# Decode attention over a 4096-token window with a gated mixer: the order of the work behind the last unit's scores

## The chip, the cores and the metric

The kernel runs on one core of one Trainium2 chip. The metric is the device time of one execution in microseconds (us). The kernel before takes 219.3 us, the median of three runs (219.18 to 219.53). A change under about 0.2% (0.44 us) can't be told from none in a measurement of this kernel.

## The reference, cut to what matters

Two batches, one new token each (B = 2, D = 512), 32 query heads on 8 key/value heads of 128 dimensions, float32 throughout. Only the last W = 4096 keys and values of each cache are read.

```python
xn = layernorm(x)
q = (xn @ wq) per head
scores = q . k[last 4096] * 128**-0.5
p = softmax(scores)
o = p @ v[last 4096]
s = o (all heads side by side, 4096) @ wo          # 4096 x 512
z = gelu(xn @ w_in); z1, z2 = halves; z2 = layernorm(z2)
g = silu((z1 * (w_sp * z2 + b_sp)) @ w_out)
out = x + s * g
```

What has to be read is some 89 MB: wq 8 MB, w_in 3.5 MB, w_out 1.8 MB, the windows of keys and of values 32 MB each, and wo 8 MB.

## The kernel before, in words

**Units.** The attention is cut into eight units: batch b (0 or 1) times four pairs of key/value heads. A unit reads 4 MB of keys and 4 MB of values, 128 partitions by 8192 numbers. The last unit (n = 7) is called `last`, and the one before it is `prev` at the end (n = 6).

**Transfers.** All large loads go through one ring of four 4-MB slots in SBUF, and all are issued by SP, in the order of a list: wq, w_in, w_out, then keys of unit n and values of unit n-1 by turns, the values of unit 7, and then wo in pieces of 16, 8, 4, 1, 1, 1 and 1 blocks (a block is 512 numbers on each partition, 256 KB). `advance(slot)` (lines 93 to 100) marks a slot free in the program and issues what now fits; the issue waits on the chip for the last reader of the place that it overwrites. The 16 blocks go to the slot of unit 5's values, the 8 to that of unit 7's keys, and the 4 and the four single ones to that of unit 6's values.

**One unit** (loop of lines 499 to 526). VectorE (DVE) turns the keys in four transposes (`turn`, tiles `kt`). `scores` makes 16 matmuls on TensorE (PE) into the PSUM bank `sh`, ScalarE (ACT) copies it to `shs`, and `by_group_of_keys` regroups it with one matmul to the bank `s`. `share_max` takes a maximum per partition on DVE (`m`, `mg`), and one small matmul spreads it over the partitions that share a head (bank `mo`); `shift` makes the negative maximum `nb` of it (`mx`, `nb`); `probs` is the exponential on ACT (`p`, with its sums); `probs_t` transposes `p` to `pT` on DVE. `weigh`, in the last unit of a batch only, makes the reciprocal sums (`ls`, `lr`, a one-column matmul into `mo`, `wd`). `values` makes 16 matmuls of `pT` with the values, four at a time in the four column groups of the array, into the bank `acc`; `scale_out` multiplies four quarters of `acc` by a mask (tile `o`, one buffer; four ACT instructions, or two on ACT and two on DVE for `last`), and `collect` adds `o` with one matmul into the bank `col` of all units.

**The program's order is each engine's order.** The wrapper `InOrder` (lines 27 to 39) keeps every engine's instructions as written, so all of them have line 37 in the profile, and tiles tell them apart. Waits between engines are put in by the framework. One float32 matmul of the program is two MATMUL rows of the trace.

**The loop is one unit behind itself**: while the keys of unit u are turned, unit u-1 goes through maximum, exponential and transpose, and its values follow the scores of u.

**The end.** After the loop, `last` goes alone through `share_max` to `weigh`. Then come the first eight of its values, `gather` (DVE sums `col` over its four column blocks to `hq`, one matmul to the bank `oT`), the other eight values, `scale_out`, `divide` (by the sums, into the tile `oT`) and `collect_last` (bank `ol`, a reduction and a division). Then the projection with wo (lines 541 to 558): 28 blocks into the bank `part`, copied by ACT to `parts`, blocks 28 and 29 into the bank `so`, `parts` spread into `so`, blocks 30 and 31 into `so`. Each piece of wo is waited for before its first block. DVE forms `res` in two steps, and SP stores it.

Of the kernel before, what the change touches and what calls it, by code (L numbers as in the profile page):

```python
# [16 lines left out]
G = 4  # L17
# [4 lines left out]
def ap(t, offset, dims):  # L22

    return bass.AP(tensor=t.tensor, offset=t.offset + offset, ap=[list(t.ap[0])] + [list(d) for d in dims])
# [18 lines left out]
def kernel(  # L43
# [15 lines left out]
    B, _, D = x.shape  # L59
# [9 lines left out]
    NU = B * HKV // 2  # L69
    J = 2 * W // P  # L70
    JC = 512 // 32
# [21 lines left out]
    def advance(*slots):  # L93
        for n in slots:
            free[n] = True
        while queue and all(free[n] for n in queue[0][1]):
            load, at = queue.pop(0)
            for n in at:
                free[n] = False
            load(ring[:, at[0] * SLOT : (at[-1] + 1) * SLOT], at[0])  # L100
# [4 lines left out]
    def bank(name, tag):  # L105
        return ps.tile([P, 512], F32, tag=tag, name=name, bufs=BANKS[tag])
# [35 lines left out]
    for n in range(NU):  # L142
        u = Unit()
# [223 lines left out]
    def form_gate():  # L367
        dve.tensor_scalar(gate, y, -1.0, 80.0, op0=ALU.mult, op1=ALU.min)
        act.activation(gate, gate, AF.Exp)
        dve.tensor_scalar_add(gate, gate, 1.0)  # L370
        dve.reciprocal(gate, gate)
        dve.tensor_mul(gate, gate, y)


    def turn(u, m):

        u.kt[m] = sb.tile([P, JC, DH], F32, tag="kt", name=f"kt{u.n}_{m}", bufs=KTB)
        dve.transpose(
            u.kt[m].rearrange("p j d -> p (j d)"), u.k[:, JC * m : JC * m + JC, :].rearrange("p j d -> p (j d)")
        )  # L380

    def scores(u):

        u.sh = bank(f"sh{u.n}", "sh")
        for dq in range(4):
            for m in range(NCH):
                pe.matmul(
                    u.sh[32 * m : 32 * m + 32, :], q_of(u, dq), u.kt[m][:, :, 32 * dq : 32 * dq + 32],
                    start=(dq == 0), stop=(dq == 3),
                )  # L390
        u.shs = sb.tile([P, 512], F32, tag="shs", name=f"shs{u.n}", bufs=1)
        act.activation(u.shs, u.sh, AF.Copy)

    def by_group_of_keys(u):

        u.s = bank(f"s{u.n}", "s")
        pe.matmul(u.s, regroup, u.shs, start=True, stop=True)

    def share_max(u):
        m2 = sb.tile([P, 2], F32, tag="m2", name=f"m2_{u.n}")  # L400
        dve.tensor_reduce(m2, ap(u.s, 0, [[1, 2], [2, 256]]), axis=AX.X, op=ALU.max)
        mg = sb.tile([P, 2, G * NCH], F32, tag="mg", name=f"mg{u.n}")
        dve.tensor_mul(mg, ap(m2, 0, [[1, 2], [0, G * NCH]]), spot.rearrange("p a g m -> p a (g m)"))
        u.mo = bank(f"mo{u.n}", "mo")
        dve.tensor_add(mg[:, 0], mg[:, 0], mg[:, 1])
        pe.matmul(u.mo[:, : G * NCH], same_r, mg[:, 0], start=True, stop=True)

    def shift(u):

        mx = sb.tile([P, 1], F32, tag="mx", name=f"mx{u.n}")  # L410
        dve.reduce_max(mx, u.mo[:, : G * NCH], axis=AX.X)
        u.nb = sb.tile([P, 2], F32, tag="nb", name=f"nb{u.n}")
        dve.scalar_tensor_tensor(u.nb, ap(mx, 0, [[0, 2]]), -SCALE, negm, op0=ALU.mult, op1=ALU.add)
# [3 lines left out]
    def probs(u):  # L417

        u.p = sb.tile([P, 512], F32, tag="p", name=f"p{u.n}")
        if u.w == 0:  # L420
            sums[u.b] = sb.tile([P, NU // B, 2], F32, tag="l", name=f"l{u.b}")
        for a in range(2):
            act.activation(
                ap(u.p, a, [[2, 256]]), ap(u.s, a, [[2, 256]]), AF.Exp,
                bias=u.nb[:, a : a + 1], scale=SCALE, accum_out=sums[u.b][:, u.w, a : a + 1],
            )

    def probs_t(u):
        u.pT = sb.tile([P, JC, 32], F32, tag="pT", name=f"pT{u.n}")
        dve.transpose(u.pT.rearrange("p j r -> p (j r)"), u.p)  # L430

    def weigh(u):

        if u.w < NU // B - 1:
            return
        ls = sb.tile([P, NU // B], F32, tag="ls", name=f"ls{u.b}")
        dve.tensor_reduce(ls, sums[u.b], axis=AX.X, op=ALU.add)
        lr = sb.tile([P, NU // B, 8, 4], F32, tag="lr", name=f"lr{u.b}")
        dve.tensor_mul(lr, ap(ls, 0, [[1, NU // B], [0, 8], [0, 4]]), ap(rowr, 0, [[0, NU // B], [1, 8], [0, 4]]))
        pe.matmul(u.mo[:, 32:33], lr.rearrange("p w r e -> p (w r e)"), ones[:, 0:1], start=True, stop=True)  # L440
        dve.reciprocal(wd[:, u.b : u.b + 1], u.mo[:, 32:33])

    def values(u, js=range(JC)):
        if js[0] == 0:
            u.acc = bank(f"acc{u.n}", "acc")
        for j in js:
            c = j % G
            pe.matmul(
                u.acc[32 * c : 32 * c + 32, :], u.pT[:, j, :], u.v[:, j : J : JC, :],
                start=(j < G), stop=(j >= JC - G),  # L450
            )

    def scale_out(u):
        u.o = sb.tile([P, 4, DH], F32, tag="o", name=f"o{u.n}", bufs=1)
        for jj in range(4):
            o, acc, m = u.o[:, jj, :], u.acc[:, jj * DH : (jj + 1) * DH], diag[:, jj : jj + 1]
            if u is units[-1] and jj >= 2:
                dve.tensor_scalar_mul(o, acc, m)
            else:
                act.activation(o, acc, AF.Copy, scale=m)  # L460
# [3 lines left out]
    def collect(u, end=NU // B - 1):  # L464

        if u.n == 0:
            col[0] = bank("col", "col")
        r = slice(32 * u.b, 32 * u.b + 32)
        pe.matmul(
            col[0][r, :], sel[:, 24 - 8 * u.w : 56 - 8 * u.w], u.o.rearrange("p j d -> p (j d)"),  # L470
            start=(u.w == 0), stop=(u.w == end),
        )

    def gather(b):

        hq = sb.tile([P, 32], F32, tag="hq", name=f"hq{b}")
        by_d = col[0][32 * b : 32 * b + 32, :].rearrange("p (j d) -> p d j", j=NCH)
        for e in range(4):
            dve.reduce_sum(hq[32 * e : 32 * e + 32, :], by_d[:, 32 * e : 32 * e + 32, :], axis=AX.X)
        t = bank(f"oT{b}", "acc")[:, :32]  # L480
        pe.matmul(t, perm, hq, start=True, stop=True)
        return t

    def divide(b, t, r=slice(0, P)):
        dve.tensor_scalar_mul(oT[r, :, 16 * b], t, wd[r, b : b + 1])
# [11 lines left out]
    last = units[-1]  # L497
    prev = None
    for u in units:
        turn(u, 0)  # L500
        if u.n == NU // B + 1:
            divide(0, gather(0))
        turn(u, 1)
        if prev is not None:
            share_max(prev)
        else:
            form_gate()
        turn(u, 2)
        if prev is not None:
            shift(prev)  # L510
            probs(prev)
        turn(u, 3)
        advance(u.slot["k"])
        if prev is not None:
            probs_t(prev)
            weigh(prev)
        scores(u)
        if prev is not None:
            values(prev, range(G))
        by_group_of_keys(u)  # L520
        if prev is not None:
            values(prev, range(G, JC))
            scale_out(prev)
            advance(prev.slot["v"])
            collect(prev, prev.w if u is last else NU // B - 1)
        prev = u
    share_max(last)
    shift(last)
    probs(last)
    probs_t(last)  # L530
    weigh(last)
    early = slice(0, 32 * last.w)
    values(last, range(8))
    t = gather(last.b)
    values(last, range(8, JC))
    scale_out(last)
    divide(last.b, t[early, :], early)
    collect_last(last)
# [52 lines left out]
```

## Time and profile before

| what | value |
|---|---|
| time, median of three runs | 219.3 us (219.18 to 219.53) |
| time of the profiled execution | 219.93 us |
| span in it, first to last instruction | 218.1 us |
| mean granted TensorE clock | 0.863 of full speed |
| PE / DVE / ACT busy | 62% / 49% / 14% of the span |
| DMA queue of SP | 95.8% of 16 engines' span, 410 GB/s over the span |

The profile shows one execution, in us from the span's start. "Idle before" is the time that an engine stood still ahead of an instruction, with what ended it. The chain of waits goes back from the last instruction to what released each step. The granted clock is the share of full speed that TensorE had; in this trace it is either 1.00 or 0.50 at any moment.

### The profile page before, as it was taken

The numbers are of one execution on the slowest core, as the hardware profiler recorded it, in microseconds if no ns is written. First come the engines' busy times: TensorE is split into PE (matmuls) and PEld (weight loads), VectorE is DVE, ScalarE is ACT, GpSimd is POOL, SyncE is SP. The second block draws the span as 40 slices with busy tenths as digits, with TensorE's granted clock in tenths as the row PEclk, the third lists the DMA queues.
The fourth block names the chain that finished last, engine by engine and source line by source line (L and its number), as shares of the span: only waits on it lengthen the run. The fifth ranks groups of instructions, "written<-read, shape, count | busy, mean of one in ns | idle before, by whom it ended". The sixth has DMA issues, their size and how long they took to land.

```text
span 218.1 us, 2001 instructions
## 1 busy us (share of the span) xinstructions
PE 134.6 (62%) x794; PEld 36.2 (17%) x794; DVE 106.8 (49%) x161; ACT 31.1 (14%) x88; POOL 4.2 (2%) x21
## 2 busy tenths in 40 slices
PE   0010895417286698697782099358869638929593
PEld 0010221111011121121210032012112111203221
DVE  1040016348685968569309904394990396122201
ACT  2030000151201102213020101201221201130101
POOL 6010000000000000000000000000000000000000
PEclk9999997966959769999997559959999957995998
DMA  9889999999999999999999998999999999999950
GB/s 385 385 385 411 442 407 453 448 409 458 409 451 415 451 415 448 409 457 403 463 400 463 403 463 385 476 391 475 388 463 403 463 403 457 406 457 394 407 224 1
DMA packets 3788, 89.52 MB, mean 410 GB/s; under 512 B 434, under 2 KB 450, under 8 KB 964
## 3 DMA queue, kind: packets, MB, share of 16 engines
q1 hardware_dynamic: 3772, 89.40, 95.8%
q8 instruction: 6, 0.10, 0.2%
q14 instruction: 2, 0.02, 0.0%
q10 hardware_dynamic: 8, 0.00, 0.0%
HBM read 89.40 MB, written 0.00 MB: 410 GB/s over the span
## 4 chain that ended last, share of the span: by engine, by line
PE 35%; DMA 31%; DVE 25%; ACT 5%; issue 2%; ACTq 0%; DVEq 0%
DMA ring<-in_A_k_cache_dram 21%; DVE kt L37 16%; DMA ring<-in_A_wq_dram 10%; PE sh L37 9%; PE acc L37 8%; PE q_ps L37 5%; PE part L37 3%; PE z L37 2%; PE s L37 2%; ACT o L37 2%; PE y L37 2%; PE col L37 1%; DVE m L37 1%; PE mo L37 1%; DVE gate L37 1%
## 5 line engine op out<-in xcount | busy, mean ns | idle before, releaser
L37 DVE STREAM_TRANSPOSE kt<-ring 128x2048 f32<-128x2048 f32 x32 | 73.0, 2297 | 35.1 <-DMA ring<-in_A_k_cache_dram 30.6
L37 PE MATMUL sh<-kt,qbd 128*32 128x512 f32 x256 | 52.3, 733 | 12.3 <-DVE kt L37 11.5
L37 PE MATMUL acc<-ring,pT 128*32 128x512 f32 x256 | 38.1, 638 | 0.0
L37 PEld LDWEIGHTS sh<-kt,qbd 128*32 128x32 f32 x256 | 10.3, 128 | 47.9 <-DVE kt L37 22.7
L37 PE MATMUL q_ps<-ring,xnT 128*32 128x512 f32 x64 | 10.0, 795 | 7.4 <-DMA ring<-in_A_wq_dram 7.4
L37 ACT ACTIVATE o<-acc,diag 128x128 f32<-128x128 f32 x30 | 8.6, 368 | 37.0 <-PE acc L37 37.0
L37 PE MATMUL col<-o,sel 128*32 128x512 f32 x14 | 7.3, 602 | 9.3 <-ACT o L37 9.3
L37 ACT ACTIVATE p<-s,nb 128x256 f32<-128x256 f32 x16 | 7.6, 488 | 37.3 <-DVE nb L37 37.3
L37 PEld LDWEIGHTS acc<-ring,pT 128*32 128x32 f32 x256 | 8.9, 114 | 20.7 <-issue 20.6
L37 ACT ACTIVATE shs<-sh 128x512 f32<-128x512 f32 x8 | 4.8, 597 | 52.0 <-PE sh L37 52.0
L37 PE MATMUL mo<-mg,same_r 128*128 128x16 f32 x16 | 3.8, 313 | 13.1 <-DVE mg L37 13.1
L37 PE MATMUL xnT_ps<-ident,xn 2*128 2x2 f32 x4 | 0.6, 252 | 14.7 <-DVE xn L37 14.7
L37 PE MATMUL s<-shs,regroup 128*128 128x512 f32 x16 | 9.0, 643 | 0.8 <-ACT shs L37 0.8
L37 DVE STREAM_TRANSPOSE qT<-q_ps 128x512 f32<-128x512 f32 x2 | 1.4, 718 | 15.5 <-PE q_ps L37 15.3
L37 DVE TENSOR_REDUCE m<-s 128x2 f32<-128x512 f32 x8 | 5.3, 666 | 6.0 <-PE s L37 6.0
L37 PE MATMUL part<-ring,oT 128*32 128x512 f32 x56 | 6.2, 594 | 0.7 <-DVE oT L37 0.7
L37 PEld LDWEIGHTS mo<-mg,same_r 128*128 128x128 f32 x16 | 3.0, 234 | 19.2 <-DVE mg L37 13.7
L37 DVE STREAM_TRANSPOSE pT<-p 128x512 f32<-128x512 f32 x8 | 5.4, 674 | 1.1 <-ACT p L37 1.1
L37 PE MATMUL mo<-ones,lr 128*128 128x1 f32 x4 | 1.2, 363 | 7.7 <-DVE lr L37 7.7
L37 PE MATMUL y<-ring,hT 128*32 128x512 f32 x14 | 3.3, 993 | 3.8 <-DVE hT L37 3.8
L37 ACT ACT_TABLE_LOAD x4 | 5.1, 1283 | 0.8 <-PEq L577 0.7
L37 PEld LDWEIGHTS q_ps<-ring,xnT 128*32 128x32 f32 x64 | 2.7, 139 | 13.9 <-issue 13.9
(114 smaller groups left out, 61.8 us busy)
## 6 DMA issues: line engine op xcount, KB each, us to landing
ring<-in_A_k_cache_dram SPq DMA_DIRECT2D x8, 4096.0 KB, 19.7
ring<-in_A_v_cache_dram SPq DMA_DIRECT2D x8, 4096.0 KB, 24.4
ring<-in_A_wo_dram SPq DMA_DIRECT2D x1, 4096.0 KB, 30.5
ring<-in_B_w_in_dram SPq DMA_DIRECT2D x1, 3584.0 KB, 16.9
ring<-in_A_wo_dram SPq DMA_DIRECT2D x1, 2048.0 KB
ring<-in_B_w_out_dram SPq DMA_DIRECT2D x1, 1792.0 KB, 20.8
ring<-in_A_wo_dram SPq DMA_DIRECT2D x1, 1024.0 KB
ring<-in_A_wo_dram SPq DMA_DIRECT2D x4, 256.0 KB, 18.8
```

Source lines behind the costliest of these rows:

```text
L37: return self.tc.keep_in_program_order(call(*args, **kwargs))
```

## The change

In the last pass of the loop, `prev`'s remaining twelve values, its scaling and its collection no longer stand inside the loop. Behind the regrouping of the last unit's scores four of these values are left, then comes `share_max(last)` to `probs(last)`, then `prev`'s last eight values and the release of its slot, then the transpose and the sums of `last`. `prev`'s `scale_out` stands behind these, and its `collect` between the first and the second eight values of `last`. `gather` moves behind the second eight.

```diff
         if prev is not None:
             values(prev, range(G))
         by_group_of_keys(u)
+        if u is last:
+            break
         if prev is not None:
             values(prev, range(G, JC))
             scale_out(prev)
             advance(prev.slot["v"])
-            collect(prev, prev.w if u is last else NU // B - 1)
+            collect(prev)
         prev = u
+    values(prev, range(G, 8))
     share_max(last)
     shift(last)
     probs(last)
+    values(prev, range(8, JC))
+    advance(prev.slot["v"])
     probs_t(last)
     weigh(last)
+    scale_out(prev)
+    values(last, range(8))
+    collect(prev, prev.w)
     early = slice(0, 32 * last.w)
-    values(last, range(8))
+    values(last, range(8, JC))
     t = gather(last.b)
-    values(last, range(8, JC))
     scale_out(last)
     divide(last.b, t[early, :], early)
     collect_last(last)
```

On PE, from the regrouping of the last unit's scores (`s_800`) to the last unit's output (`ol`), before (`acc_795` is the bank of `prev`, `acc_847` that of `last`, `mo_829` with 16 columns the maximum, with one column the sums):

```order
L37 MATMUL s_800<-shs_793,regroup 128x512
L37 MATMUL acc_795<-ring,pT_774 32x512 x12
L37 MATMUL col<-o_814,sel 32x512
L37 MATMUL mo_829<-mg_827,same_r 128x16
L37 MATMUL mo_829<-ones,lr_843 128x1
L37 MATMUL acc_847<-ring,pT_839 32x512 x8
L37 MATMUL oT_861<-hq_856,perm 128x32
L37 MATMUL acc_847<-ring,pT_839 32x512 x8
```

The same place in the changed kernel (`acc_795` is still `prev`, `acc_846` is `last`):

```order
L37 MATMUL s_800<-shs_793,regroup 128x512
L37 MATMUL acc_795<-ring,pT_774 32x512 x4
L37 MATMUL mo_810<-mg_808,same_r 128x16
L37 MATMUL acc_795<-ring,pT_774 32x512 x8
L37 MATMUL mo_810<-ones,lr_837 128x1
L37 MATMUL acc_846<-ring,pT_833 32x512 x8
L37 MATMUL col<-o_841,sel 32x512
L37 MATMUL acc_846<-ring,pT_833 32x512 x8
L37 MATMUL oT_869<-hq_864,perm 128x32
```

The matmul of the maximum now stands behind four of `prev`'s values where it stood behind twelve and the collection; the collection stands between the two halves of `last`'s values, and the matmul of `gather` behind both.

On ACT, from the copy of the last unit's scores on (`p` is the exponential of `last`, `o` from `acc_795` the scaling of `prev`):

```order
 L37 ACTIVATE shs_793<-sh_776 128x512
-L37 ACTIVATE o_814<-acc_795,diag 128x128 x4
-L37 ACTIVATE p_836,l_626<-s_800,nb_834 128x256 x2
-L37 ACTIVATE o_871<-acc_847,diag 128x128 x2
+L37 ACTIVATE p_817,l_626<-s_800,nb_815 128x256 x2
+L37 ACTIVATE o_841<-acc_795,diag 128x128 x4
+L37 ACTIVATE o_871<-acc_846,diag 128x128 x2
```

The exponential of `last` now stands ahead of `prev`'s scaling. The order on DVE, POOL and SP stays as it was.

## The prediction

> **What bounds the kernel now.** I read the page's slices first, then the transfers at the end, then the chain of waits backwards from the store, then the granted clock by windows. DMA's row of the page:
>
> ```profile
> DMA  9889999999999999999999998999999999999950
> ```
>
> The DMA engines are busy in 38 of 40 slices, so the transfers set when everything arrives. The question is how much work is left behind the last of them. First a window at the end (columns: stretch, its us, busy us of PE, PEld, DVE, ACT, POOL, clock, DMA share, GB/s), then SP's issues with their times, each followed by the row of the transfers that gives its us from issue to landing (the values of unit 7, and four loads of wo):
>
> ```profile
> 212.00:213.00 1.00, 1.00 (x16) 0.26 (x8) 0.00 (x0) 0.00 (x0) 0.00 (x0) 1.00 0.00 0
> ```
>
> ```profile
> L37 SPq DMA_DIRECT2D ring<-in_A_v_cache_dram x1: 535/535/535, 163.3 to 163.3; - x1
> ring<-in_A_v_cache_dram SPq DMA_DIRECT2D x1, 4096.0 KB, 29.1
> 171.60 0.33 SPq L37 DMA_DIRECT2D ring<-in_A_wo_dram  x1
> ring<-in_A_wo_dram SPq DMA_DIRECT2D x1, 4096.0 KB, 30.5
> 191.19 11.21 SPq L37 DMA_DIRECT2D ring<-in_A_wo_dram  x5
> L37 SPq DMA_DIRECT2D ring<-in_A_wo_dram x2: 424/428/432, 192.0 to 192.5; - x2
> ring<-in_A_wo_dram SPq DMA_DIRECT2D x2, 256.0 KB, 18.8
> L37 SPq DMA_DIRECT2D ring<-in_A_wo_dram x1: 328/328/328, 202.1 to 202.1; - x1
> ring<-in_A_wo_dram SPq DMA_DIRECT2D x1, 256.0 KB, 10.0
> ```
>
> So unit 7's values are there at 163.3 + 29.1 = 192.4, the first 16 blocks of wo at 171.6 + 30.5 = 202.1, and the last block at 202.1 + 10.0 = 212.1. The two single blocks before it land 18.8 behind 192.0 and 192.5, at 210.8 and 211.3. The row of five at 191.19 begins with the pieces of 4 and 1 and ends with the issue at 202.1. Between 202.1 and 210.8 the engines carry 8 + 4 + 2 blocks, 3.7 MB, at a nearly even rate; my estimate by bytes is 207.0 for the piece of 8 and 209.5 for the piece of 4. Now the longest steps of the chain of waits from 188 on (start, us, what):
>
> ```profile
> 188.41 2.76 PE acc L37 x24
> 191.25 1.15 ACT o L37 x4
> 192.45 1.04 PE col L37 x2
> 193.49 0.34 PE mo L37 x2
> 194.26 1.03 ACT p L37 x4
> 195.31 0.71 DVE pT L37
> 196.45 0.59 PE mo L37 x2
> 197.03 3.57 PE acc L37 x16
> 200.60 0.57 PE oT L37 x2
> 201.17 2.73 PE acc L37 x16
> 203.98 0.63 ACT o L37 x2
> 204.64 0.62 DVE o L37 x2
> 205.40 1.05 PE ol L37 x8
> 207.11 6.26 PE part L37 x56
> 213.39 0.61 ACT parts L37
> 214.04 0.91 PE so L37 x24
> ```
>
> No step here is a transfer. The projection starts at 207.11, just when its second piece has come, takes 7.84 to the end of `so` at 214.95, and ends 2.9 behind the last landing. That is all that a reordering of this tail can win, less the work on the last block.
>
> The Trainium skill, "Perfetto Trace Analysis", section "Identifying Performance Opportunities", says that improving a kernel means improving its most contended engine. That is the DMA here, which the change doesn't touch, and by that rule the sum would be zero, 219.9 in the profiled execution. The window from 212 disagrees: PE is busy in all of it, and no byte moves.
>
> The clock of the tail, by windows cut where it changes, with three earlier ones ahead to compare:
>
> ```profile
> 124.30:131.12 6.82, 5.72 (x30) 1.77 (x34) 1.18 (x5) 0.00 (x0) 0.00 (x0) 0.50 1.04 447
> 161.84:165.25 3.41, 1.98 (x21) 0.68 (x24) 1.99 (x2) 0.24 (x2) 0.00 (x0) 1.00 1.07 461
> 178.91:182.32 3.41, 3.41 (x6) 0.18 (x2) 3.38 (x4) 1.03 (x4) 0.00 (x0) 0.50 1.01 432
> 192.56:195.98 3.42, 1.26 (x4) 0.32 (x3) 1.00 (x4) 1.02 (x4) 0.00 (x0) 1.00 0.93 402
> 195.98:199.39 3.41, 2.94 (x14) 1.09 (x18) 1.68 (x8) 0.00 (x0) 0.00 (x0) 0.50 1.00 432
> 199.39:202.80 3.41, 3.41 (x18) 0.90 (x14) 0.00 (x0) 0.00 (x0) 0.00 (x0) 0.50 0.94 400
> ```
>
> PE is busy 1.26 of 3.42 us in the window to 195.98, and the clock is 0.50 in the next two windows; with 1.98 of 3.41 busy (161.84) it stayed at 1.00. It came back at 182.32 and at 202.80, each time behind a window that was busy throughout. That is why 16 rows of `acc` took 3.57 at 197.03, where 24 took 2.76 at 188.41.
>
> **The change part by part.** All times are on the scale of the profiled execution. DVE's timeline gives when the maximum is ready, and `hq`:
>
> ```profile
> 188.45 0.69 DVE L37 TENSOR_REDUCE m<-s 128x2 f32<-128x512 f32 x1 [5.04 <-PE s L37]
> 189.18 0.19 DVE L37 TENSOR_TENSOR mg<-m,spot 128x32 f32<-128x32 f32 x1
> 189.40 0.18 DVE L37 TENSOR_TENSOR mg<-mg 128x16 f32<-128x16 f32 x1
> 193.85 0.17 DVE L37 TENSOR_REDUCE mx<-mo 128x1 f32<-128x16 f32 x1 [4.28 <-PE mo L37]
> ...
> 197.27 1.18 DVE L37 TENSOR_REDUCE hq<-col 32x32 f32<-32x128 f32 x4
> ```
>
> *The maximum earlier.* Four values (8 rows, 2.76 x 8/24 = 0.92) run from 188.41 to 189.3, under the reductions that end at 189.58. The maximum's matmul (0.34) starts there and ends at 189.98, and `mx` starts at 190.0 where it started at 193.85: -3.85. What comes off the path is twelve values less that cover, the four scalings (1.15) and the collection (1.04). If the four values ran longer than the reductions the loss would be some tenths.
>
> *Exponential to sums.* From `mx` to the one-column matmul is 196.45 - 193.85 = 2.60, so that starts at 192.6. Under it PE makes `prev`'s other eight values (16 rows, 1.84) from 190.0 to 191.9; they cost nothing as long as they end before 192.6, and beyond it each us costs one. ACT now has the exponential first (done at about 191.4) and then the four scalings of `prev`, 191.9 to 193.1.
>
> *The last unit's values.* The one-column matmul (0.34 at full clock, as the 16-column one) ends at 192.9, behind the landing of unit 7's values at 192.4: those can wait no earlier. Eight values take 1.84, to 194.8, instead of 3.57. The collection follows; its input is ready since 193.1, so it waits for nothing (cover 1.7) and adds its 1.04 to this path, to 195.8. Eight values more end at 197.6. That this runs at full clock follows from the windows: PE stands still for 0.3 and 0.7 between 189 and 197.6, which leaves every 3.4-us window busier than the 1.98 that sufficed. If it were half anyway, this stretch would last up to 4.9 longer.
>
> *Gather.* `hq` now waits for the collection: 195.8 + 1.18 = 197.0, before `last`'s scaling on DVE needs the engine. Its matmul runs on PE under ACT's scaling, so 0.57 leaves the path. Queued behind `hq` on DVE are only that scaling and the divisions.
>
> *From there* the rows repeat: the scaling starts at 197.65 instead of 203.98, -6.3, and `part` could start at 207.11 - 6.3 = 200.8. Before any transfer is asked, the gain is 6.3: 3.85 from the order, 2.5 from the clock and the shorter row of matmuls.
>
> *The transfers take most of it back.* The first 16 blocks come at 202.1, so PE stands still for 1.3. 32 rows of `part` at 6.26/56 each take 3.6, to 205.7; the piece of 8 comes at 207.0 and takes 1.8, to 208.8; the piece of 4 comes at 209.5 and takes 0.9, to 210.4; blocks 28 and 29 come at 210.2 and 210.8; `parts` (0.61) is there at 211.1 and spread by 211.5; block 30 at 211.3, block 31 at 212.1. Behind that eight rows of `so` remain, for which 24 rows took 0.91: about 0.45 with the latency of a row. `so` ends at 212.5 instead of 214.95: **-2.45**. This has slack: `part` could start as late as 204.5 with the same end, so 3.7 of the 6.3 could fail.
>
> *Releasing the slot later.* SP's row of five issues at 191.19 waits for `prev`'s last values, which end at 191.9 instead of 191.1. The engines reach these bytes only behind the piece of 8, at about 207, so 0.8 costs nothing; it would cost from a delay of some 15. The last issue, at 202.1, waited for the landing of the 16 blocks, not for PE, and stays. `o` has one buffer: `last`'s scaling must wait for `prev`'s collection, done 1.8 earlier.
>
> *The unknown cost: the clock in the projection.* No row shows a projection that waits for pieces. `ol` is busy 1.05 of the 4.5 us between 197.6 and 202.1, so a window that ends there is as idle as the one to 195.98, and the clock may fall to half just before `part`. From below it costs nothing: at half clock PE no longer waits for pieces, and by the windows it comes back after at most two (6.8 us) when PE works without pause. From above, 6.8 us at half lose 3.4 of work: 202.1 + 6.26 + 3.4 = 211.8 for `part`, 212.4 for `parts`, then the spread and blocks 30 and 31, 213.1. So the end lies between 212.5 and 213.1, and I take 212.5, since most positions of the windows let the clock return by 208.
>
> The Trainium skill, "TensorE: Matmul & The Clock Gate", section "Part 1: The HAM clock gate", gives half rate after at least one idle window of about 3.4 us. By that the pauses here (2.0 and 1.3) are too short, and the sum is 212.5; the row to 195.98 fell with 1.26 us busy, so the trace speaks for the harsher reading, 213.1 at worst.
>
> **The sum.** Profiled: 219.93 - 2.45 = 217.5, to 218.1 with the slow projection. The median of the runs is 0.63 below the profiled execution. If that is the cost of profiling, it comes off as well: 216.9. If other executions had the half clock for less of the tail (one window less is worth 1.7), it doesn't, because the changed end hangs on the transfers: 217.5. I take 217.3.
>
> **Rivals.**
>
> *The projection at half clock for two windows* (above): the idle stretch ahead of `part` speaks for it, that PE works without pause afterwards speaks against its lasting. 217.5 to 218.1.
>
> *No gain.* The last landing goes later by what the tail got earlier, because the four last issues stand behind a wait that moved. Against it: the DMA queue has 15 us of work ahead at 191.9. It would take landings at 214.5: 219.3.
>
> *Slower: the clock stays at half through the whole projection.* Pieces that come one by one could leave no window busy throughout. Then 56 rows take 12.5 from 202.1, to 214.6, `parts` 215.25, and 24 rows of `so` at half about 1.3: 216.55, +1.6, a time of 220.9 to 221.5. It decides from the point where half clock lasts over (214.95 - 209.9) x 2 = 10.1 us behind 202.1, 209.9 being 202.1 + 7.84. The window 124.30 to 131.12 speaks against it: there the clock came back once PE had work without pause, and at half clock the pieces are there before PE asks.
>
> *The change doesn't bring the maximum forward*, because something else than PE's order held it back. The row `mo` at 193.49 followed `col` without a pause, while `mg` had been done since 189.58, so it was the order. Even if only 2.6 of 6.3 came, the end would be the same.
>
> **How the numbers follow.** Transfers end the kernel at full or nearly full clock: 0.67, at 216.9 to 217.6. Slow projection: 0.24, 217.5 to 218.1. No gain: 0.05, about 219.3. Slower: 0.04, about 221. The range 216.7 to 218.3 holds the first two with a little for the landing, which may differ by 0.2. Faster by over 0.2% (0.44 us, what a measurement can tell from no change): 0.91; within: 0.05; slower: 0.04.
>
> **What would show it.** Right: `mx` of the last unit near 190.0; no half clock between 189 and 197; `acc` of `last` in two runs of about 1.8; `part` idle before with a DMA of wo as its releaser; a chain that ends in the landing of wo's last block and `so` some 0.45 behind it; the last landing still at 212.1. Wrong: a chain through `part` without a DMA, a last landing beyond 212.5, or a granted clock of 0.50 beyond 209.

## The result, and the profile after

The changed kernel takes 217.44 us, the median of six runs (217.27 to 217.60); its time over that of the kernel before is 0.9908, with a 95% interval of 0.9893 to 0.9923. Of the six executions of the kernel before beside it, four take 219.18 to 219.87; two that lie far above, at 223.24 and 230.57, are left out of the ratio. The profiled execution takes 217.38 us with a span of 215.6, against 219.93 and 218.1 before. The forecast was 217.3, and 217.5 by the sum on the profiled scale.

The DMA engines' row of its page:

```profile
DMA  9898999999999999999999999999999999999990
```

They are now busy in 39 of 40 slices. The chain of waits from the last maximum on (start, us, what, its longest steps):

```profile
189.80 0.40 PE mo L37 x2
190.20 1.90 PE acc L37 x16
192.11 17.32 DMA ring<-in_A_wo_dram
209.48 1.11 PE part L37 x8
210.61 0.60 ACT parts L37
211.26 0.64 PE so L37 x16
211.92 0.47 PE so L37 x8
```

Behind the maximum nothing of the last unit stands in the chain any more: the piece of four blocks, issued at 192.11 when `prev`'s values had been read, lands at 209.43, and then come eight rows of `part`, the copy, the spread and the last block. PE's timeline of the same stretch shows where the last unit went (the bracket is the idle time before the row, with what ended it):

```profile
190.13 1.92 PE L37 MATMUL acc<-ring,pT 128*32 128x512 f32 x16
192.90 0.38 PE L37 MATMUL mo<-ones,lr 128*128 128x1 f32 x2 [0.85 <-DVE lr L37]
193.21 2.33 PE L37 MATMUL acc<-ring,pT 128*32 128x512 f32 x17
...
199.25 1.03 PE L37 MATMUL ol<-o,sel 128*32 128x128 f32 x8 [1.21 <-DVE o L37]
202.03 2.53 PE L37 MATMUL part<-ring,oT 128*32 128x512 f32 x12 [1.75 <-DMA ring<-in_A_wo_dram]
```

`ol` runs at 199.25 where it ran at 205.40, and PE stands for 1.75 us ahead of `part`, until the first 16 blocks of wo have landed. The clock (columns as in the prediction) of three windows, cut where the clock can change:

```profile
198.95:202.36 3.41, 1.36 (x12) 0.98 (x16) 0.88 (x4) 0.00 (x0) 0.00 (x0) 1.00 0.90 381
202.36:205.77 3.41, 3.41 (x20) 1.09 (x16) 0.00 (x0) 0.00 (x0) 0.00 (x0) 0.50 0.98 416
205.77:209.18 3.41, 3.32 (x32) 0.92 (x24) 0.00 (x0) 0.00 (x0) 0.00 (x0) 1.00 0.97 384
```

The half clock hasn't gone: it has moved from the last unit's values (195.98 to 202.80 before) to the first blocks of the projection, and lasts one window there. It costs nothing, since PE has caught up with the transfers by 209.1 and waits again for the landing at 209.43.

### The profile page after: what moved, and what is told of

Read it like the earlier page. It is cut to its first block, busy times and chain, and to the rows that moved or that the text cites. A ratio compares the mean times of both kernels' runs of the same rounds, so it can differ in the third digit from the quotient of the medians.

```text
span 215.6 us, 2002 instructions
## 1 busy us (share of the span) xinstructions
PE 133.5 (62%) x794; PEld 36.1 (17%) x794; DVE 106.7 (49%) x161; ACT 31.1 (14%) x88; POOL 4.2 (2%) x21
## 4 chain that ended last, share of the span: by engine, by line
DMA 40%; PE 29%; DVE 25%; ACT 4%; issue 1%; DVEq 0%; ACTq 0%
DMA ring<-in_A_k_cache_dram 22%; DVE kt L37 17%; DMA ring<-in_A_wq_dram 10%; PE sh L37 9%; DMA ring<-in_A_wo_dram 8%; PE acc L37 5%; PE q_ps L37 5%; PE z L37 2%; PE s L37 2%; PE y L37 2%; DVE m L37 1%; ACT o L37 1%; PE yq L37 1%; PE col L37 1%; DVE mg L37 1%
## 5 line engine op out<-in xcount | busy, mean ns | idle before, releaser
L37 PE MATMUL sh<-kt,qbd 128*32 128x512 f32 x256 | 50.9, 707 | 12.7 <-DVE kt L37 11.8
L37 PE MATMUL acc<-ring,pT 128*32 128x512 f32 x256 | 36.4, 596 | 0.0
L37 PE MATMUL part<-ring,oT 128*32 128x512 f32 x56 | 8.1, 729 | 2.1 <-DMA ring<-in_A_wo_dram 2.1
```

The costliest lines, as they stand in the source:

```text
L37: return self.tc.keep_in_program_order(call(*args, **kwargs))
```

## The experiments

The theory: the end hangs on the landings of wo, and any tail that is early enough meets them. The main rival: the tail's own chain still sets the end, and the gain is the sum of what each part of the change took off it. Each ratio is to the kernel before, run beside the experiment. The experiments ran on three chips, where the kernel before has medians of 219.39 to 219.85, so differences of some tenths between medians of different experiments say little.

**The kernel before with a busy PE.** Nothing is moved; eight matmuls whose result isn't used stand in the pause between the maximum's matmul and the sums.

```diff
     share_max(last)
+    busy = bank("busy", "sh")
+    for j in range(8):
+        c = j % G
+        pe.matmul(busy[32 * c : 32 * c + 32, :], rowm, last.shs, start=(j < G), stop=(j >= 4))
     shift(last)
```

> The kernel before with eight matmuls (result unused) on PE in its pause behind the maximum's matmul, about 1.9 of the 2.6 us; nothing is moved. Theory: the window that had 1.26 of 3.42 us busy has about 3.1, the clock stays at full, the last unit's values take 1.85 instead of 3.57, part starts near 204.3 instead of 207.1 and the end meets the landings at 212.5: 217.4 to 217.8. Rival (only the new order brings the gain): 219.3 to 219.9. If the clock falls for another reason, the granted clock shows it.

Measured: 217.48 us (217.38 to 217.57), ratio 0.9910 (0.9885 to 0.9935), the same as the changed kernel. PE's timeline of it:

```profile
193.61 0.40 PE L37 MATMUL mo<-mg,same_r 128*128 128x16 f32 x2
193.93 1.92 PE L37 MATMUL busy<-shs,rowm 128*32 128x512 f32 x16
196.65 0.38 PE L37 MATMUL mo<-ones,lr 128*128 128x1 f32 x2 [0.79 <-DVE lr L37]
196.96 1.92 PE L37 MATMUL acc<-ring,pT 128*32 128x512 f32 x16
...
204.33 6.21 PE L37 MATMUL part<-ring,oT 128*32 128x512 f32 x56 [0.68 <-DVE oT L37]
```

The maximum's matmul is as late as before, but the last values take 1.92 where they took 3.57, and `part` starts at 204.33, as expected. The clock is at full throughout the tail, and the chain ends, as in the next experiment, in the landing of the last block at 211.9. So the half clock of the last unit's values was by itself worth all that could be won. The reordering isn't needed for the gain; not letting the clock fall is enough, if only just: `part` starts 0.3 before the latest start that costs nothing (204.6, worked out below).

**One part alone: the maximum early.** Scaling and collection stay ahead of the last unit's values, `gather` stays in the middle.

```diff
     values(prev, range(8, JC))
     advance(prev.slot["v"])
+    scale_out(prev)
     probs_t(last)
     weigh(last)
-    scale_out(prev)
-    values(last, range(8))
     collect(prev, prev.w)
     early = slice(0, 32 * last.w)
-    values(last, range(8, JC))
+    values(last, range(8))
     t = gather(last.b)
+    values(last, range(8, JC))
```

> One part of the change alone: the maximum behind four of the preceding unit's values, but scaling and collection ahead of the last unit's values as before, gather in the middle as before. Theory: col waits for the scaling until about 193.4, the last values start near 194.4 instead of 193.2, part could start near 201.6, before the first 16 blocks are there; the whole gain remains, 217.4 to 217.6. Rival (both parts add up to the gain): about half is lost, 218.4 to 218.7.

Measured: 217.46 us (217.42 to 217.56), ratio 0.9909 (0.9887 to 0.9932). The whole gain, as the theory has it. The chain's last steps are two loads of wo and eight rows:

```profile
171.98 29.99 DMA ring<-in_A_wo_dram
201.97 0.02 issue
201.99 9.96 DMA ring<-in_A_wo_dram
211.95 0.04 issue
212.00 0.47 PE so L37 x8
```

The row of 29.99 is the piece of 16 blocks, whose landing lets SP issue the last block; that lands 9.96 later. Neither depends on the order that the change touches.

**The other part alone: the collection late.** The maximum stays behind all of `prev`'s values.

```diff
-    values(prev, range(G, 8))
+    values(prev, range(G, JC))
     share_max(last)
     shift(last)
     probs(last)
-    values(prev, range(8, JC))
     advance(prev.slot["v"])
```

> The other part alone: the maximum behind all of the preceding unit's values, scaling and collection behind the last unit's first values. Theory: the maximum's matmul starts near 191.4 instead of 189.8, the chain is 1.6 later, part could start near 202.6, inside the slack of 3.7: 217.4 to 217.7, and up to 0.5 more if the longer pause of PE drops the clock in the values. Rival (parts add up): about 218.5.

Measured: 218.64 us (217.49 to 219.19), ratio 0.9957 (0.9937 to 0.9977): about half of the gain, so this looks like the rival's figure. The windows and the chain tell it apart:

```profile
190.84:194.26 3.42, 1.32 (x14) 0.38 (x6) 0.88 (x3) 1.60 (x7) 0.00 (x0) 1.00 1.02 441
194.26:197.67 3.41, 2.82 (x14) 1.09 (x18) 0.67 (x4) 0.46 (x2) 0.00 (x0) 0.50 0.98 423
197.67:201.09 3.42, 3.42 (x20) 0.76 (x16) 0.34 (x2) 0.00 (x0) 0.00 (x0) 0.50 0.94 399
```

```profile
195.43 4.40 PE acc L37 x17
199.84 0.85 PE acc L37 x3
...
205.93 6.26 PE part L37 x56
212.21 0.61 ACT parts L37
212.86 0.91 PE so L37 x24
```

With the maximum late, nothing is left for PE to do between the maximum and the sums, the window to 194.26 has 1.32 us of work, and the clock is half for two windows. From the matmul of the sums to `ol` it takes 9.37 (194.85 to 204.22) where the changed kernel takes 6.35 (192.90 to 199.25), `part` starts at 205.93 instead of the 202.6 that I expected, and the end at 213.77 is the tail's own. My expectation allowed 0.5 for the clock; it cost 3.0 us on the way to `part`, of which the slack hides more than half: `so` ends 1.4 behind the changed kernel. The two runs with nearly the whole gain, 217.49 and 217.55, are those with the highest mean clock of the twelve, 0.873 and 0.869; nine of the other ten have 0.858 or 0.859, and one window at half clock changes the mean by 3.41 x 0.5 / 217 = 0.008. But the tenth, with 0.867, is the slowest of all, 219.19: the mean over the whole span doesn't say where the half clock lay.

**The landings taken away.** Both kernels load only four blocks of wo and use them eight times. A small load of x that is tied to the sixteenth block is tied to the fourth here; the diff leaves this line out.

```diff
-    for piece in ((16,), (8,), (4, 1, 1, 1, 1)):
+    for piece in ((4,),):
         enqueue(load_blocks(piece))
...
-        t, a = blocks[n]
+        t, a = blocks[n % 4]
```

> The changed kernel loads only four blocks of wo and projects with these eight times over, so that no transfer is left behind the values of unit 7 but 1 MB; the output is another. Theory: part starts where its chain lets it, near 200.9, and the span ends 7.84 + 3.2 behind it: so ends at 208.7, 3.7 before the changed kernel, time 213.7, up to 1.7 more with a window of half clock. Rival (something else than the transfers holds the end at 212.4): 217.4.

Measured: 215.47 us (214.00 to 216.62), ratio 0.9801 (0.9738 to 0.9863); the profiled execution is the one of 214.00. Its chain:

```profile
200.98 6.26 PE part L37 x56
207.26 0.61 ACT parts L37
207.91 0.91 PE so L37 x24
```

`part` starts at 200.98, where the sum of the prediction had 200.8 before any transfer was asked, and `so` ends at 208.82. So in the changed kernel 3.6 us of the earlier tail are indeed kept back by the landings. The four runs are 214.00, 214.33, 216.61 and 216.62. The two slower ones lie 2.3 to 2.6 above the others, more than the 1.7 that the prediction gives a window of half clock; no profile of such a run was taken, and the cause stays open.

> The kernel before with the same cut to four blocks of wo; the output is another. Theory: its end never waited for a transfer, so the time stays at 219.3 to 219.9, and the difference to the cut changed kernel, 5.6 to 6.2, is what the order alone is worth. Rival (the kernel before is held by the transfers too): it gets faster by 2 or more.

Measured: 219.72 us (219.06 to 220.25), ratio 0.9994 (0.9977 to 1.0010). The kernel before never waited for these landings. Between the two cut kernels lie 4.25 by medians and 5.16 by the profiled executions, under the 5.6 to 6.2 expected. The two slower runs of the cut changed kernel pull the medians together; and the profiled execution of the cut kernel before had the half clock for one window, not two:

```profile
197.07:200.48 3.41, 3.41 (x18) 0.64 (x17) 1.30 (x5) 0.00 (x0) 0.00 (x0) 0.50 0.00 0
200.48:203.90 3.42, 2.40 (x22) 0.71 (x18) 0.23 (x1) 0.62 (x2) 0.00 (x0) 1.00 0.00 0
```

**More work behind the last landing.** The last eight blocks of wo come in one load instead of five.

```diff
-    for piece in ((16,), (8,), (4, 1, 1, 1, 1)):
+    for piece in ((16,), (8,), (8,)):
```

> The changed kernel with the last eight blocks of wo in one load of 2 MB where there were five (1 MB and four of 256 KB). Theory: the last landing stays near 211.8 or up to 0.4 earlier, but behind it stand eight rows of part (1.1), parts (0.6), the spread and blocks 30 and 31 (0.9) instead of eight rows of so (0.5): so ends near 214.0, time 218.8 to 219.3. Rival (PE's chain sets the end, not the landing): 217.4.

Measured: 219.77 us (219.59 to 221.37), ratio 1.0030 (1.0009 to 1.0052), so 2.3 us over the changed kernel. The chain:

```profile
192.07 19.75 DMA ring<-in_A_wo_dram
211.86 1.11 PE part L37 x8
213.00 0.61 ACT parts L37
213.65 0.91 PE so L37 x24
```

The load lands at 211.82, as the single block does, and 2.7 us of work stand behind it instead of 0.5. The end moves with what hangs on the last landing. The time is 0.5 above my range: my own terms, 211.8 with 1.1, 0.6 and 0.9, give 214.4 for the end of `so` and not 214.0, and it is 214.55. Four of the ten runs, at 220.32 to 221.37, are slower still, and no trace shows why.

**The slack.** The changed kernel with 8 (called e1) or 24 DVE multiplications (result unused) ahead of the last division, and then with 8 and 16 of them together with 12 and 24 matmuls that keep PE busy in that pause. The diff shows 8 with 12 matmuls; the first two kernels have the multiplications alone.

```diff
         dve.reduce_sum(ol[r, :], t.rearrange("p (j n) -> p n j", j=NCH), axis=AX.X)
+        idle = sb.tile([P, P], F32, tag="idle", name="idle")
+        for _ in range(8):
+            dve.tensor_mul(idle, ident, ident)
+        busy = bank("busy", "sh")
+        for j in range(12):
+            c = j % G
+            pe.matmul(busy[32 * c : 32 * c + 32, :], rowm, u.shs, start=(j < G), stop=(j >= 12 - G))
         divide(u.b, ol[r, :], r)
```

> The changed kernel with eight multiplications on DVE (128x128, result unused) between the reduction of ol and the last division, about 2.3 us on the chain that leads to the projection. Theory (the landings of wo set the end, part has 3.7 us of slack of which 1.2 is the wait for the first 16 blocks): part starts near 203.2, so still ends near 212.4, time 217.4 to 217.7. Rival (the tail's own chain sets the end): the delay arrives in full, 219.7.

Measured: 219.19 us (218.07 to 219.60), ratio 0.9969 (0.9949 to 0.9989). A miss: the delay, 2.6 us where 2.3 was expected, was to be free, and cost 0.6 to 2.2 in the runs. The windows and the chain of the profiled execution, of 219.60:

```profile
199.35:202.76 3.41, 1.00 (x8) 0.73 (x8) 2.16 (x8) 0.00 (x0) 0.00 (x0) 1.00 0.95 400
202.76:206.17 3.41, 2.58 (x15) 0.61 (x18) 0.73 (x3) 0.00 (x0) 0.00 (x0) 0.50 0.94 396
```

```profile
203.59 9.22 PE part L37 x56
```

`part` starts at 203.59, inside the slack, but the pause has made the clock fall, for two windows (to 209.59), and `part` takes 9.22 instead of 6.26.

> The same with 24 multiplications, about 7 us. Theory: beyond the slack the delay counts; part starts at 200.9 + 7 = 207.9 and needs 7.84 at full clock, so ends at 215.7, which is 3.3 later than the changed kernel: 220.7, and up to 1.7 more where the pause drops the clock for a window. Rival (the tail's chain sets the end): 217.4 + 7 = 224.4.

Measured: 224.32 us (223.42 to 225.12), ratio 1.0206 (1.0169 to 1.0243). This is the rival's figure, and over the theory's. In its profile the clock is half from 201.61 to 215.26, four windows, `part` starts at 209.45 (the multiplications took 0.33 each) and takes 9.13; 209.45 + 7.84 + 5.81 / 2 for the half clock gives the end of `so` at 220.2 that is measured. By its time alone this run can't tell the theories apart, so the delay was repeated with PE kept busy.

> The changed kernel with the eight DVE multiplications of e1 (2.6 us) and twelve matmuls on PE (result unused) in the pause that they make ahead of part. In e1 the clock was half from 202.76 to 209.59 and part took 9.22 instead of 6.26. Theory (the delay itself fits into the slack, its cost there was the clock): the clock stays at full, part starts near 203.6, so ends near 212.5, time 217.4 to 217.6. Rival (the slack was mis-sized and the delay counts by itself): 218.5 to 219.6 as in e1.

Measured: 217.70 us (217.51 to 217.86), ratio 0.9919 (0.9892 to 0.9947). The same delay is now free within 0.3: `part` starts at 203.52 and the chain ends in the landing again:

```profile
201.92 9.95 DMA ring<-in_A_wo_dram
211.92 0.47 PE so L37 x8
```

> The same with sixteen multiplications (5.2 us) and 24 matmuls in the pause. Theory: part starts near 206.2 at full clock and needs 7.84 to the end of so, 214.0, which is 1.6 behind the changed kernel: 219.0. Rival (as long as PE is kept busy the landings alone set the end): 217.5.

Measured: 219.40 us (219.00 to 219.97), ratio 0.9998 (0.9983 to 1.0013); the profiled execution has 219.06. With the double delay the tail's chain is the longer one:

```profile
206.19 6.26 PE part L37 x56
212.47 0.61 ACT parts L37
213.12 0.91 PE so L37 x24
```

`part` starts at 206.19 and `so` ends at 214.03, 1.6 behind the changed kernel. So at full clock `part` may start 206.19 - 1.6 = 204.6 at the latest; the prediction had 204.5. The slack is there, but only for a PE that doesn't pause.

## Why the prediction was right

- *What bounds the kernel.* That 2.9 us of work stood behind the last landing, and that this, less the work on the last block, limits the gain, is shown from both sides: without the landings the changed kernel is faster still (215.47), the kernel before isn't (219.72), and three different ways to an earlier tail (the change, the early maximum, the busy PE) all end within 217.44 to 217.48.
- *The maximum earlier.* `mx` was to start at 190.0 and starts at 190.2; the scores of that execution came 0.17 later.
- *The last unit's values.* At full clock as forecast: the 32 rows and the collection run from 193.21 to 197.70 without a pause, `ol` at 199.25, 6.15 before its old place (6.3 forecast).
- *The transfers take most back.* `part` starts with the 16 blocks at 202.03 (202.1 forecast), waits for the piece of four at 209.43 (209.5), and `so` ends at 212.39 (212.5). The gain on the profiled scale is 2.55 against 2.45. The sign "a chain that ends in the landing of wo's last block" isn't in this profile, whose chain goes through the piece of four; it is in those of the early maximum, of the busy PE and of the busy delay of 2.6, where the last block landed at 211.9. Here the spread ends at 211.90, and the weight load of the last block, at 211.91, waited for a DMA: the two paths are a tie.
- *Releasing the slot later.* SP's issue moved from 191.19 to 192.11 without effect: the piece landed at 209.43, 209.5 forecast.
- *The unknown cost.* The clock did fall ahead of `part`, as the row to 195.98 let expect; it came back after one window, and its price was at the lower bound, nothing. At half clock PE no longer waited for the piece of eight, as the prediction said. The Trainium skill, "TensorE: Matmul & The Clock Gate", section "Part 1: The HAM clock gate", asks for an idle window of 3.4 us; here the window to 202.36 had 1.36 us of work and a pause of 1.75, so the measurement decides for the harsher reading, that a whole idle window isn't needed.
- *The profiled execution and the median.* The 0.63 between them didn't come off: the changed kernel's median (217.44) is its profiled time (217.38). The sum, 217.5, was the better number; the 217.3 lay between two readings of the 0.63, and that it still came within 0.14 is luck. That speaks against a cost of profiling and for the clock, but doesn't show it: over the 23 runs that the kernel before had beside some of the experiments it spreads from 218.60 to 220.25, 1.65, about the 1.7 that one window was priced at, while the kernels that end in the landing (the change, the early maximum, the busy PE, the busy delay of 2.6) spread 0.1 to 0.4. But the kernel with one load for the last eight blocks ends behind a landing too and spreads 1.8. Nor can it be read run by run: of the other runs only the mean clock over the whole span is known, and that doesn't sort them (of the 23, the two with 0.875 take 219.39 and 219.48, the fastest, 218.60, has 0.866).

Two steps were wrong. "This has slack: `part` could start as late as 204.5 with the same end, so 3.7 of the 6.3 could fail" holds at full clock only. A tail that is later by waiting lets the clock fall, and then the projection needs up to 3 us more: the delay of 2.6, with `part` at 203.59, lost up to 2.2. And "Even if only 2.6 of 6.3 came, the end would be the same" was the cover for a maximum that isn't brought forward. The experiment with the late maximum is that case, and only 1.2 came (`part` at 205.93), not the 4.5 of its order: the pause stayed, and the clock fell in it.

Also the share of 3.85 for the order and 2.5 for the clock says less than it seems: the clock alone is enough, as the busy PE shows. The order alone would be enough by the sum (207.11 - 3.85 = 203.3), but that isn't shown: where the maximum came early, `prev`'s values also filled PE's pause, and what the new order would bring if the clock fell all the same was not tried.

## What to carry to other kernels

Where transfers run without a gap, look for the work behind the last landing: its length, less what the last piece itself needs, is the most that a reordering can win, and a tail that is earlier than that only waits. Before moving work to shorten a tail, see whether a pause of PE lets its clock fall there; filling the pause with work from elsewhere, or with idle matmuls, can be the whole gain. A slack that is reckoned at full clock isn't one against a pause.

## What the runs showed of the hardware

- From one change of the clock to the next lie 3.41 us or a multiple of it, in all twelve traces.
- It fell behind windows in which PE was busy 1.00, 1.26, 1.32 or 1.36 us, none of them idle throughout, and stayed at full with 1.98. Between these the busy time of a window doesn't decide it. With one load for the last eight blocks the clock stayed at full behind 1.82 and 1.60, around a pause of 3.13 us (the first two rows); in the kernel with the early maximum, earlier in the span, it fell behind 1.85 (the next two), and in the one with 24 multiplications behind 1.58 (198.19 to 201.61). What else counts stays open.

```profile
206.91:210.32 3.41, 1.82 (x16) 0.31 (x15) 0.00 (x0) 0.00 (x0) 0.00 (x0) 1.00 0.81 341
210.32:213.74 3.42, 1.60 (x28) 0.73 (x32) 0.00 (x0) 0.60 (x1) 0.00 (x0) 1.00 0.07 29
68.13:71.54 3.41, 1.85 (x7) 0.74 (x8) 2.87 (x5) 0.11 (x1) 0.00 (x0) 1.00 1.07 461
71.54:74.95 3.41, 2.97 (x6) 0.18 (x2) 3.31 (x4) 1.02 (x4) 0.00 (x0) 0.50 1.05 452
```

- In the tails it came back behind half windows that were busy throughout; 2.58, 2.82 and 2.94 of 3.41 were followed by a second one. That isn't a rule either. In the cut kernel before, earlier in the span, 3.00 wasn't enough and 2.85 was (each row with the window behind it):

```profile
125.39:128.80 3.41, 3.00 (x14) 1.09 (x18) 0.49 (x3) 0.00 (x0) 0.00 (x0) 0.50 1.07 461
128.80:132.21 3.41, 3.41 (x20) 0.79 (x16) 0.00 (x0) 0.00 (x0) 0.00 (x0) 0.50 1.05 452
180.00:183.41 3.41, 2.85 (x10) 0.38 (x10) 3.38 (x5) 1.02 (x4) 0.00 (x0) 0.50 1.07 461
183.41:186.82 3.41, 3.41 (x33) 0.94 (x26) 0.25 (x1) 0.00 (x0) 0.00 (x0) 1.00 1.02 437
```

- Matmuls whose result nobody reads kept the clock at full in two kernels: eight of them in a pause made the kernel before 0.9% faster (219.50 to 217.48), and twelve made a delay of 2.6 us free.
